# Routed experts: the first expert's weight remainders and token remainders placed anew on VectorE

## The chip, the cores and the metric

One core of a Trainium2 chip runs the whole program. The metric is the device time of one execution in microseconds (us); lower is better. The engines are TensorE (PE in the rows, with PEld for its weight loads), VectorE (DVE), ScalarE (ACT), GpSimd (POOL) and SyncE (SP), each with its own queue of instructions that runs in order.

## The reference

Sliding-window attention (8 batches, 8 heads, 576 positions, head size 64, window 64), and on its output a layer of 8 experts. Every expert takes exactly `cap` tokens, in the order of all token and expert scores:

```python
    logits = x @ w_gate
    order = np.argsort(-logits.flatten())
    for idx in order:
        tok, e = (int(idx) // E, int(idx) % E)
        if assigned[tok] >= 0 or counts[e] >= cap:
            continue
        assigned[tok] = e
        counts[e] += 1
...
    for e in range(E):
        mask = assigned == e
        h = np.maximum(x[mask] @ w1[e], 0.0)
        out[mask] = h @ w2[e]
```

There are N = 4608 tokens of D = 512, E = 8 experts with F = 1024 hidden values, and cap = 576.

## The kernel before

Attention runs first, to about 148 us. Then three streams of work share the engines. *Routing* finds, for one expert after another (position p = 0 to 7), which expert fills up next and the list of its 576 tokens: choice steps on VectorE (`choices`, L454 to L461), eight rounds of comparisons with thresholds (`compare`, L469) and counting matmuls (L538 for p = 0, L554 for later p), and then a list of token numbers, `idx` (L758). *Loading* brings the weights of expert p as eight tiles of 128 x 1024, four of w1 and four of w2 (`load`). *Products* are the matrix products.

Products are made to nearly float32 precision with numbers of a shorter kind (fp32r): each operand is a rounded part (`wh` for weights, `xh` for tokens, `hh` for hidden values) and a remainder (`wl`, `xl`, `hl`), and a product takes three matmuls, high by high, low by high and high by low. ScalarE makes the rounded parts (L899, L1002, L1156). The token and hidden remainders are subtractions on VectorE (L1006, L1161). A weight remainder is made in one of two ways: by a subtraction on VectorE (L903), or by ScalarE writing the negated rounded part (L908) and a DMA from GpSimd's queue that adds the weights to it in memory (L910). In expert 0 the first three tiles go the first way and the other five the second; experts 1 to 5 go the second way throughout.

The tokens of an expert are gathered from the attention's output by five indirect DMAs of GpSimd (L1012), four of 128 tokens and one of 64. TensorE transposes each gathered tile (L936), and ScalarE and VectorE make `xh` and `xl` of it. The first products are units: 128 hidden values by 256 or 320 tokens, twelve matmuls into one of three PSUM buffers (L1188), four of `wh` by `xh`, four of `wl` by `xh`, four of `wh` by `xl`. Expert 0 starts with six units on its first 256 tokens, which need token tiles 0 and 1; units 1 and 2 use weight tile 0, units 3 and 4 tile 1, units 5 and 6 tile 2. The second products (L1227, L1235) follow, and the results are scattered by GpSimd (L1217).

The order of all instructions is fixed while the kernel is built, by a planner with a clock of its own (`Streams`). Every stream is a generator; what it yields is a planned delay or a condition on which it is held, and it issues instructions when its time has come. `busy(dt, eng)` adds a planned duration to an engine's planned end and returns how far that end lies ahead. Routing paces itself on VectorE by

```python
    def dve(self, dt):
        return self.busy(0.4 * dt, "dve") + 0.6 * dt
```

so a routing step waits for all that is planned on VectorE, and each choice step is `yield self.dve(490)`. In the same clock (ns) a weight remainder on VectorE is 1130, a token remainder 600, a unit of 256 columns 1440, and a hidden remainder 335. The real engines follow the planned order, each at its own speed. With Z for the planner's time at which the first list is there, before the change: the gathers are issued at Z; the three weight tiles of expert 0 are converted at Z, Z+1.15 and Z+2.30 us and their remainders issued 1.05 after each; the transposes of token tile 0 are issued at Z+4.18 and of tile 1 at Z+5.46, `xh` 1 at Z+5.89 and `xl` 1 at Z+6.59.

The clock of TensorE has two levels here, and sparse work after attention leaves it on the lower one; `warm` issues matmuls whose results nobody uses (dummies): 28 behind the last step of the first list (L476, called at the end of `steps`), and 6 between the transposes of token tiles 0 and 1.

Of the kernel before, what the change touches and what calls it, by code (L numbers as in the profile page):

```python
# [9 lines left out]
FT = mybir.dt.float32  # L10
FR = mybir.dt.float32r
# [3 lines left out]
AF = mybir.ActivationFunctionType  # L15
OP = mybir.AluOpType
# [344 lines left out]
class Routing:  # L361
# [132 lines left out]
    def steps(self, p):  # L494

        nc, wk, V = self.nc, self.wk, self.V
# [6 lines left out]
        if p < E - 1:  # L503
# [19 lines left out]
            for r in range(NR):  # L523
# [18 lines left out]
                else:  # L542
# [22 lines left out]
                    st = self.st[0:M]  # L565
# [186 lines left out]
            for h in range(2):  # L752
                nc.tensor.matmul(ip[32 * g:32 * g + 32], ils[:, :, h], self.s5[:, h, g], start=(h == 0), stop=(h == 1))
        if p == 0:
            self.warm(28)
        yield self.busy(100) + 200 + slack
        idx = self.rt.tile([128, 5], U32, name=f"idx{p}")
        nc.vector.tensor_copy(idx, ip)  # L758
# [2 lines left out]
        if p < E - 1:  # L761
            if not p:
                nc.vector.scalar_tensor_tensor(self.eid, m, T[:, 0:1], best, op0=OP.is_gt, op1=OP.mult)
            eq = tile_([128, NJ], FT, name="eq", bufs=1)
            nc.vector.scalar_tensor_tensor(eq, Y[:, 1], CAP + 0.5, X[:, 1], op0=OP.is_lt, op1=OP.mult)  # L765
            nc.vector.scalar_tensor_tensor(self.eid, eq, code[:, 0:1], self.eid, op0=OP.mult, op1=OP.add)
            nc.vector.tensor_scalar(self.un, self.eid, 0.0, None, op0=OP.is_equal)
            yield self.dve(400)
            e1 = tile_([128, E], FT, name="e1")
            nc.vector.tensor_scalar(e1, self.cw, code, -FAR, op0=OP.is_equal, op1=OP.mult)  # L770
            nc.vector.tensor_tensor(V, V, e1[:, None, :].to_broadcast([128, NJ, E]), OP.add)
            yield self.dve(600)

            nc.vector.scalar_tensor_tensor(self.oh, m[:, :, None].to_broadcast([128, NJ, E]), T[:, 0:1], one,
                                           op0=OP.is_gt, op1=OP.mult)
            c2 = tile_([128, E], BF, name="c2")
            with nc.allow_low_precision(reason="whole numbers up to 36"):
                nc.vector.tensor_reduce(c2, self.oh.rearrange("p j e -> p e j"), axis=AX.X, op=OP.add)
            yield self.dve(900)

            def taken():
                cn = self.room(128, E)
                nc.tensor.matmul(cn, self.ones, c2, start=True, stop=True)
                yield self.busy(110) + 200 + slack
                nc.vector.tensor_tensor(self.left, self.left, cn, OP.add)
                e2 = tile_([128, E], FT, name="e2")
                nc.vector.tensor_scalar(e2, self.cw, code, -1.0e6, op0=OP.is_equal, op1=OP.mult)
                nc.vector.tensor_tensor(self.left, self.left, e2, OP.add)
                yield self.dve(500)

            self.taken = taken
            if not p or p == E - 2:
                yield slack if p < OWN else 1500
                yield from taken()

    def expert(self, p, code):
        ei = self.rt.tile([1, 1], I32, name=f"ei{p}")
# [19 lines left out]
class Experts:  # L817
# [30 lines left out]
    def load(self, p, ei):  # L848

        nc, fw = self.nc, self.fw  # L850
        yield lambda: self.taken == self.pairs[p]
        e = nc.sync.value_load(ei[0:1, 0:1], min_val=0, max_val=E - 1)
        eg = nc.gpsimd.value_load(ei[0:1, 0:1], min_val=0, max_val=E - 1) if p == 0 else None
        st, there = {}, {}

        def fetch(i):
            st[i] = fw.tile([128, 1024], FT, name="st", bufs=STAGE)

            q, r = (nc.gpsimd, eg) if p == 0 and i >= 4 else (nc.sync, e)
            q.dma_start(st[i], self.part(i, r))  # L860

            there[i] = max(self.clock(), there.get(i - 1, 0)) + \
                (LOAD if p else 1500) * (1 if i else 2)
            if q is nc.gpsimd:
                there[i] = max(there[i], self.clock() + self.busy(600, "pool") + 4700)

        ahead = 2 if p in SEVEN else 3 if p else 4
        for i in range(ahead):
            fetch(i)
        if p == 0:  # L870
            yield lambda: self.gathered

        def sums(x, y):
            w = x.rearrange("p (k c h f) -> p k c h f", k=2, c=2, h=2)
            s = y.rearrange("p (s c f) -> p s c f", s=4, c=2)
            tt = nc.vector.tensor_tensor
            for d, a, b, op in ((s[:, 0], w[:, 0, :, 1], w[:, 1, :, 1], OP.add),
                                (s[:, 2], w[:, 0, :, 0], w[:, 0, :, 1], OP.subtract),
                                (s[:, 1], s[:, 0], w[:, 0, :, 0], OP.subtract),
                                (s[:, 3], w[:, 1, :, 0], s[:, 1], OP.subtract)):  # L880
                tt(d, a, b, op)
                yield self.busy(350, "dve")

        seven = p in SEVEN
        jobs = [(i, k) for i in range(2 * NCH) for k in range(2 if seven and i < NCH else 1)]
        for i, k in jobs:
            if p == 0 and i == 3:
                yield lambda: self.tiles[0] > 1
            yield lambda: self.taken - self.ring < self.used
            if there[i] > self.clock():  # L890
                yield there[i] - self.clock()
            x = st[i]
            if k:
                x = fw.tile([128, 1024], FT, name="st", bufs=STAGE)
                yield from sums(st[i], x)
                yield 150
            hi = fw.tile([128, 1024], FR, name="wh", bufs=self.ring)
            lo = fw.tile([128, 1024], FR, name="wl", bufs=self.ring)
            nc.scalar.activation(hi, x, AF.Copy)  # L899
            yield self.busy(970, "act") + 80  # L900
            yield lambda: self.gathered > p
            if k and i < NCH - 1 or self.quick(p, i):
                nc.vector.tensor_tensor(lo, x, hi.bitcast(FT), OP.subtract)  # L903
                self.W[p, i, k] = (hi, lo)
                dt = self.busy(1130, "dve")
            else:

                nc.scalar.activation(lo, hi.bitcast(FT), AF.Copy, scale=-1.0)  # L908
                yield self.busy(970, "act") + 180
                nc.gpsimd.dma_start(lo.bitcast(FT), x, accum_op=OP.add)  # L910
                self.spawn(self.ready((p, i, k), hi, lo), self.busy(650, "pool") + ADDED - 1200)
                dt = 1300
            self.taken += 1
            if not k and i + ahead < 2 * NCH:
                fetch(i + ahead)
            yield max(100, dt - 1200) if p or i < 3 else 900
# [392 lines left out]
def body(tc, q, k, v, vt, wg, w1, w2, xs, out):  # L1309
    nc = tc.nc  # L1310
    with ExitStack() as ctx:
        cp = ctx.enter_context(tc.tile_pool(name="cp", bufs=1))
        ctx.enter_context(tc.manual_schedule())
        c = dict(identr=cp.tile([128, 128], FR, name="identr"))
        L = cp.tile([128, NJ, E], FT, name="L")
        rt = Routing(ctx, tc, c, L)
        with ExitStack() as actx:
            ap = actx.enter_context(tc.tile_pool(name="ap", bufs=1))
            c.update(consts(tc, ap))
            wgs = ap.tile([128, HP, 32], FT, name="wgs")  # L1320
            attention(actx, tc, c, q, k, v, vt, (wgs, wg), xs, L, lambda j0, j1: rt.choices(j0, j1, 0), rt.setup,
                      rt.counters)
        rt.start()
        ex = Experts(ctx, tc, c, xs, w1, w2, out)
        rt.spare = ex.room

        st = Streams()
        ex.spawn, ex.busy, rt.busy = st.add, st.busy, st.busy
        ex.clock = rt.clock = lambda: st.now
        ex.warm, ex.rows, rt.prime = rt.warm, rt.rows, ex.prime  # L1330

        def route():
            for p in range(E):
                for dt in rt.steps(p):
                    if p in rt.eint and p not in known:
                        known.add(p)
                        st.add(ex.load(p, rt.eint[p]))
                    if p in rt.idx and p not in listed:
                        listed.add(p)
                        st.add(ex.turn(p, rt.idx[p]))  # L1340
                    yield dt

        def products():
            for p in range(E):
                yield lambda: p in ex.XT
                yield from ex.steps(p, rt.idx[p])

        known, listed = set(), set()
        st.add(route())
        st.add(products())  # L1350
        st.run()
# [17 lines left out]
```

## Time and profile before

| what | us |
|---|---|
| median of 3 runs | 645.47 |
| lowest and highest run | 643.06, 645.69 |
| profiled execution, its time | 642.53 |
| profiled execution, its span | 640.8 |
| TensorE busy | 605.8 |
| VectorE busy | 460.5 |
| mean granted TensorE clock | 0.978 of full |

The span goes from the first to the last instruction of the profiled execution; its time also holds what lies around that. Busy time of TensorE is modelled, since matmuls overlap: a busy stretch is not a stretch at its peak. Idle time in brackets stands ahead of an instruction, with what ended it.

### The profile page before, as it was taken

The page shows a single profiled execution, that of the slowest core. Times are in us where ns is not written, and L with a number is a line of the kernel's source. Part 1 is how long each engine was busy: PE and PEld are TensorE (multiplying, and loading weights), DVE is VectorE, ACT ScalarE, POOL GpSimd, SP SyncE. Part 2 cuts the span into 40 slices and gives each one's busy share as a digit, 9 for nine tenths or more (in the row PEclk, how much of TensorE's full clock was granted, in tenths as well). Part 3 has the DMA queues.
Part 4 walks back from the last instruction along what each step waited for, and adds up shares of the span by engine and source line. Part 5 has one row for each costly group of instructions (what it writes and reads, how often), then busy time and mean ns, then how long its engine had stood idle before and what let it go on. Part 6 is the DMA issues. An engine that isn't in the chain of part 4 may idle for free. (4 is left out here: it accounts for less than half of the span.)

```text
span 640.8 us, 16975 instructions
## 1 busy us (share of the span) xinstructions
PE 605.8 (95%) x6423; PEld 523.7 (82%) x6423; DVE 460.5 (72%) x2036; ACT 340.7 (53%) x596; POOL 219.3 (34%) x231
## 2 busy tenths in 40 slices
PE   7899999995599999999999999999999999999995
PEld 6787887784489779978997898799789879889984
DVE  6887888877787768875877786778777954975610
ACT  2476677671255177255646448176437545666720
POOL 4454656450142062133306215132321515123211
PEclk9999999997599999999999999999999999999998
DMA  9997969991376098779669578868929828666711
GB/s 316 368 379 280 362 245 336 373 352 53 134 236 136 18 310 198 148 255 214 156 201 236 171 145 283 196 142 275 215 82 228 208 75 223 185 159 156 162 54 41
DMA packets 39761, 133.06 MB, mean 208 GB/s; under 512 B 5112, under 2 KB 5240, under 8 KB 39680
## 3 DMA queue, kind: packets, MB, share of 16 engines
q0 software_dynamic: 14992, 51.93, 35.0%
q1 hardware_dynamic: 24400, 79.52, 34.3%
q8 instruction: 51, 0.84, 0.5%
q10 hardware_dynamic: 288, 0.52, 0.3%
q14 instruction: 30, 0.25, 0.1%
HBM read 82.15 MB, written 18.87 MB: 158 GB/s over the span
## 5 line engine op out<-in xcount | busy, mean ns | idle before, releaser
L1217 POOL DMA_INDIRECT out<-ot,idx x40 | 41.3, 1033 | 197.0 <-ACT ot L1202 61.9
L1235 PE MATMUL o<-wh,hh 128*128 128x512 f32 x256 | 102.3, 400 | 0.4 <-ACT ot L1202 0.4
L1235 PE MATMUL o<-wl,hh 128*128 128x512 f32 x256 | 101.7, 397 | 0.0
L1235 PE MATMUL o<-wh,hl 128*128 128x512 f32 x256 | 101.2, 395 | 0.0
L144 POOL TENSOR_TENSOR st<-st,mx 128x512 f32<-128x512 f32 x72 | 73.4, 1040 | 67.1 <-DVE mx L137 60.5
L899 ACT ACTIVATE wh<-st 128x1024 fp32r<-128x1024 f32 x72 | 75.7, 1052 | 11.4 <-DMA st<-w 5.3
L910 POOL DMA_DIRECT2D wl<-st x59 | 54.4, 1091 | 70.9 <-ACT wl L908 47.7
L1156 ACT ACTIVATE hh<-h 128x256 fp32r<-128x256 f32 (+1 forms) x96 | 38.9, 407 | 65.7 <-PE h L1188 64.0
L1188 PE MATMUL h<-xh,wh 128*128 128x320 f32 (+1 forms) x384 | 69.9, 301 | 0.7 <-ACT xh L1002 0.7
L1188 PE MATMUL h<-xh,wl 128*128 128x320 f32 (+1 forms) x384 | 70.5, 299 | 0.0
L1188 PE MATMUL h<-xl,wh 128*128 128x320 f32 (+1 forms) x384 | 69.7, 299 | 0.4 <-DVE xl L1006 0.4
L137 DVE CUSTOM_DVE_ANT_0 st<-Sp,mask 128x128 f32<-128x128 f32 x288 | 67.1, 283 | 3.0 <-PE Sp L128 2.4
L1012 POOL DMA_INDIRECT xg<-xs,idx x40 | 44.0, 1100 | 72.0 <-DVE eq L765 62.0
L908 ACT ACTIVATE wl<-wh 128x1024 fp32r<-128x1024 f32 x59 | 62.3, 1056 | 0.8
L1202 ACT ACTIVATE ot<-o 128x512 f32<-128x512 f32 x34 | 20.3, 597 | 75.0 <-PE o L1235 63.5
L1188 PEld LDWEIGHTS h<-xh,wh 128*128 128x128 f32 x384 | 56.8, 189 | 1.4 <-ACT xh L1002 0.8
L1188 PEld LDWEIGHTS h<-xl,wh 128*128 128x128 f32 x384 | 56.9, 189 | 0.8 <-DVE xl L1006 0.6
L1188 PEld LDWEIGHTS h<-xh,wl 128*128 128x128 f32 x384 | 56.9, 189 | 0.2
L1235 PEld LDWEIGHTS o<-wh,hh 128*128 128x128 f32 x256 | 48.1, 188 | 10.5 <-ACT ot L1202 0.8
L1235 PEld LDWEIGHTS o<-wh,hl 128*128 128x128 f32 x256 | 48.1, 188 | 9.3
L1235 PEld LDWEIGHTS o<-wl,hh 128*128 128x128 f32 x256 | 48.2, 188 | 8.8
L152 ACT ACTIVATE pt<-Tp 128x512 f32<-128x512 f32 x72 | 39.7, 594 | 19.4 <-PE Tp L150 18.3
(237 smaller groups left out, 1255.0 us busy)
## 6 DMA issues: line engine op xcount, KB each, us to landing
st<-w SPq DMA_DIRECT2D x60, 512.0 KB, 6.4
wl<-st POOLq DMA_DIRECT2D x59, 512.0 KB, 6.1
V<-v SPq DMA_DIRECT2D x16, 584.0 KB, 9.3
xs<-x SPq DMA_DIRECT2D x36, 256.0 KB, 4.5
VT<-vt SPq DMA_DIRECT2D x8, 640.0 KB, 10.1
VT<-vt SPq DMA_DIRECT2D x8, 512.0 KB, 8.3
Q<-q SPq DMA_DIRECT2D x6, 640.0 KB, 6.8
K<-k SPq DMA_DIRECT2D x6, 640.0 KB, 7.8
```

The costliest lines, as they stand in the source:

```text
L137: nc.vector.tensor_tensor_reduce(st[:, h, :], Sp[h % 2][:, h // 2], mk, scale=-0.125, scalar=3.0e38, op0=OP.add, op1=OP.min, accum_out=mx[ ...
L144: nc.gpsimd.tensor_tensor(st, st, mx[:, :, None].to_broadcast([128, 4, 128]), OP.subtract)
L152: nc.scalar.activation(pt, Tp, AF.Exp, scale=-1.0)
L899: nc.scalar.activation(hi, x, AF.Copy)
L908: nc.scalar.activation(lo, hi.bitcast(FT), AF.Copy, scale=-1.0)
L910: nc.gpsimd.dma_start(lo.bitcast(FT), x, accum_op=OP.add)
L1012: nc.gpsimd.indirect_dma_start(out=g[0:n, a], out_offset=None, in_=self.xs, in_offset=IndirectOffsetOnAxis(ap=idx[0:n, a:a + 1], axis=0))
L1156: nc.scalar.activation(hh[:, f, c0:c1], h, AF.Relu)
L1188: nc.tensor.matmul(h, wv[:, cc, 128 * (f % 2):128 * (f % 2) + 128], xt[:, cc, c0:c1], start=(k == 0), stop=(k == 11))
L1202: nc.scalar.activation(ot, o, AF.Copy)
L1217: nc.gpsimd.indirect_dma_start(out=self.out, out_offset=IndirectOffsetOnAxis(ap=idx[0:m, a:a + 1], axis=0), in_=ot[0:m], in_offset=None)
L1235: nc.tensor.matmul(o, ht[:, f, 128 * a:128 * a + 128], wt[:, 512 * (f % 2):512 * (f % 2) + 512], start=(f == 0 and k == 0), stop=(f == NF ...
```

## The change

It touches only what happens around the start of expert 0. In `load`, weight tiles 0 and 1 of expert 0 get a piece of their own: both are converted on ScalarE, tile 1 first and then tile 0, without waiting between them; the remainder of tile 0 is issued on VectorE when the gathers have been issued, that of tile 1 a planned microsecond after the `xl` of the second token tile (`lows[0] > 1`). The loop then goes on with tile 2, so its conversion and its remainder come later too; tile 3 no longer waits for the second token tile. Routing is held, at the end of p = 0, on the condition `settled`, which is the same `lows[0] > 1`: the choice steps for expert 1 are issued behind the `xl` of the first two token tiles. And the dummies behind the first list go from 28 to 25.

```diff
--- before.py
+++ after.py
@@ -752,7 +752,7 @@
             for h in range(2):
                 nc.tensor.matmul(ip[32 * g:32 * g + 32], ils[:, :, h], self.s5[:, h, g], start=(h == 0), stop=(h == 1))
         if p == 0:
-            self.warm(28)
+            self.warm(25)
         yield self.busy(100) + 200 + slack
         idx = self.rt.tile([128, 5], U32, name=f"idx{p}")
         nc.vector.tensor_copy(idx, ip)
@@ -792,6 +792,8 @@
             if not p or p == E - 2:
                 yield slack if p < OWN else 1500
                 yield from taken()
+            if not p:
+                yield self.settled
 
     def expert(self, p, code):
         ei = self.rt.tile([1, 1], I32, name=f"ei{p}")
@@ -883,9 +885,27 @@
 
         seven = p in SEVEN
         jobs = [(i, k) for i in range(2 * NCH) for k in range(2 if seven and i < NCH else 1)]
+        if p == 0:
+            jobs = jobs[2:]
+            yield max(0, there[1] - self.clock())
+            hi, lo = ({}, {})
+            for i in (1, 0):
+                hi[i] = fw.tile([128, 1024], FR, name="wh", bufs=self.ring)
+                lo[i] = fw.tile([128, 1024], FR, name="wl", bufs=self.ring)
+                nc.scalar.activation(hi[i], st[i], AF.Copy)
+                yield self.busy(970, "act") + 80
+            yield lambda: self.gathered
+            for i in (0, 1):
+                if i:
+                    yield lambda: self.lows[0] > 1
+                    yield 1000
+                nc.vector.tensor_tensor(lo[i], st[i], hi[i].bitcast(FT), OP.subtract)
+                self.W[p, i, 0] = (hi[i], lo[i])
+                self.busy(1130, "dve")
+                self.taken += 1
+                fetch(i + ahead)
+                yield 100
         for i, k in jobs:
-            if p == 0 and i == 3:
-                yield lambda: self.tiles[0] > 1
             yield lambda: self.taken - self.ring < self.used
             if there[i] > self.clock():
                 yield there[i] - self.clock()
@@ -1322,7 +1342,7 @@
                       rt.counters)
         rt.start()
         ex = Experts(ctx, tc, c, xs, w1, w2, out)
-        rt.spare = ex.room
+        rt.spare, rt.settled = ex.room, lambda: ex.lows[0] > 1
 
         st = Streams()
         ex.spawn, ex.busy, rt.busy = st.add, st.busy, st.busy
```

## Rows read from the trace of the kernel before

**Rows 1.** The page, busy time of TensorE: us, share, instructions
```profile
PE 605.8 (95%) x6423; PEld 523.7 (82%) x6423; DVE 460.5 (72%) x2036; ACT 340.7 (53%) x596; POOL 219.3 (34%) x231
```

**Rows 2.** Timeline of TensorE, 172 to 187: start, us, line, operation, count, idle before
```profile
172.80 4.84 PE L476 MATMUL rps<-r,ones 128*128 128x288 bf16 x28
177.70 0.17 PE L783 MATMUL rps<-c,ones 128*128 128x8 bf16 x1
178.12 0.52 PE L936 MATMUL tp<-identr,xg 128*128 128x128 f32 x4 [0.26 <-DMA xg<-xs,idx]
...
180.36 0.74 PE L1188 MATMUL h<-xh,wh 128*128 128x256 f32 x4 [0.69 <-ACT xh L1002]
180.94 0.64 PE L1188 MATMUL h<-xh,wl 128*128 128x256 f32 x4
182.01 0.39 PE L1188 MATMUL h<-xl,wh 128*128 128x256 f32 x1 [0.44 <-DVE xl L1006]
...
186.54 0.43 PE L554 MATMUL rps<-G,one 128*32 128x60 bf16 x9
```

**Rows 3.** Timeline of VectorE over the same stretch
```profile
174.48 1.22 DVE L903 TENSOR_TENSOR wl<-st,wh 128x1024 fp32r<-128x1024 f32 x1
...
178.32 1.22 DVE L903 TENSOR_TENSOR wl<-st,wh 128x1024 fp32r<-128x1024 f32 x1
179.46 0.44 DVE L454 TENSOR_REDUCE m<-L 128x36 f32<-128x288 f32 x1
...
181.28 0.68 DVE L1006 TENSOR_TENSOR xl<-tp,xh 128x512 fp32r<-128x512 f32 x1
...
184.33 0.47 DVE L469 TENSOR_TENSOR G<-m,tab 128x300 bf16<-128x300 f32 x1
```

**Rows 4.** Timeline of ScalarE, the second first-expert weight tile
```profile
174.69 1.06 ACT L899 ACTIVATE wh<-st 128x1024 fp32r<-128x1024 f32 x1 [0.24 <-DMA st<-w]
```

**Rows 5.** Timeline of GpSimd: gathers of expert 0, then of expert 1
```profile
174.70 1.83 POOL L1012 DMA_INDIRECT xg<-xs,idx  x1 [0.30 <-issue]
...
229.88 1.01 POOL L1012 DMA_INDIRECT xg<-xs,idx  x1 [3.45 <-DVE eq L765]
...
236.26 1.02 POOL L910 DMA_DIRECT2D wl<-st  x1
```

**Rows 6.** Timeline of TensorE where expert 0 ends and expert 1 begins
```profile
242.05 0.79 PE L936 MATMUL tp<-identr,xg 128*128 128x128 f32 x8
242.67 0.47 PE L1235 MATMUL o<-wh,hl 128*128 128x512 f32 x1
...
243.44 0.43 PE L554 MATMUL rps<-G,one 128*128 128x60 bf16 x9
...
244.03 0.63 PE L1188 MATMUL h<-xh,wh 128*128 128x256 f32 x4
244.50 0.64 PE L1188 MATMUL h<-xh,wl 128*128 128x256 f32 x4
```

**Rows 7.** DMA issues from 236.0 to 236.9: engine, count, size, us to landing
```profile
wl<-st POOLq DMA_DIRECT2D x1, 512.0 KB, 4.8
```

**Rows 8.** Windows of 1 us: busy PE, PEld, DVE, ACT, POOL, clock, DMA
```profile
148.00:149.00 1.00, 0.00 (x0) 0.09 (x1) 0.86 (x7) 0.05 (x1) 0.00 (x0) 1.00 0.06 23
...
150.00:151.00 1.00, 0.00 (x0) 0.00 (x0) 0.90 (x6) 0.00 (x0) 0.00 (x0) 1.00 0.47 184
...
152.00:153.00 1.00, 0.25 (x5) 0.10 (x1) 0.56 (x3) 0.00 (x0) 0.00 (x0) 0.50 0.00 0
...
174.00:175.00 1.00, 1.00 (x6) 0.64 (x5) 0.96 (x3) 0.76 (x2) 0.69 (x2) 0.50 0.95 365
175.00:176.00 1.00, 1.00 (x8) 0.73 (x7) 1.00 (x2) 0.78 (x2) 1.00 (x1) 0.82 1.02 418
```

**Rows 9.** Timeline, GpSimd and TensorE, where expert 2 begins
```profile
290.26 3.75 POOL L910 DMA_DIRECT2D wl<-st  x4
...
302.30 0.64 PE L1188 MATMUL h<-xh,wh 128*128 128x256 f32 x4
```

## Prediction, made before the changed kernel ran

> **What bounds the kernel.** I read the page first, then the timeline of each engine from the first expert's token list to the end of its products, then the joints between experts. TensorE is busy 605.8 of 640.8 us [rows 1], and behind the wait before 182.01 its timeline marks none up to 245, through the joint of experts 0 and 1 [rows 2, 6]. So a microsecond that TensorE loses or wins between 172 and 245 reaches the end of the kernel nearly whole, and one that another engine wins is worth nothing unless TensorE was waiting for it.
>
> The reader should see three things. First, the start: 28 dummies run to about 177.64, the matmul of L783 follows, and the transposes of the first token tile wait for the gather to land at 178.12, with 0.26 us idle; then TensorE waits 0.69 us for `xh` and later for `xl` [rows 2]. Second, what makes `xl` late: VectorE does the third weight remainder at 178.32 and the first choice step of expert 1 at 179.46, and comes to the second `xl` only at 181.28 [rows 3]. Third, the joint: expert 1's first unit starts at 244.03, and its weight remainder, needed at 244.50, was sent off by GpSimd at 236.26, right behind the five gathers that began at 229.88 [rows 5, 6]. It took 4.8 us [rows 7], so it lay there at 241.1, with 3.4 us to spare.
>
> **The change, part by part.**
>
> *Fewer dummies.* 28 dummies take 4.84 us, 0.173 each; three fewer end 0.52 us sooner. Behind them stand L783 and the first transposes, which wait for the gather anyway [rows 2]. The 0.26 us of idle time becomes some 0.8. Cost and gain 0, if the clock stays up. The clock is at half speed at 174, and 0.82 in the mean from 175 to 176, behind the 28 dummies and what ran before them [rows 8]; three dummies from the end still leave more than a microsecond of work after it rose. I take 0. The other bound: if the clock fell, a stretch at half speed like that of the dummies (172.80 until within 175 to 176) would cost half its length, 1.1 to 1.6 us.
> The Trainium skill, "TensorE: Matmul & The Clock Gate", section "Why this matters for your kernels", says that gaps of idle time between matmul bursts put TensorE back to the half clock, which speaks against fewer dummies. The trace agrees in kind: TensorE did nothing in two of the three microseconds from 148 to 151 at clock 1.00, and was at 0.50 from 152 to 153 [rows 8]. By the rule the sum would be up to 1.6 us worse; by the rows on the dummies, 0.
>
> *First weight tiles.* ScalarE now converts tile 1 first (it starts at 174.69, when the tile is there [rows 4]) and tile 0 after it, 1.06 us each, so `wh` 0 is ready at 176.8 instead of 174.5 and its remainder runs from about 176.9 to 178.1. The first use of `wl` is 180.94 [rows 2]: hidden, with 2.8 us to spare. In VectorE's queue only the counting of L785 to L788 stands behind it, which nobody near waits for.
> The second gather took 1.83 us beside a weight remainder at 174.48; the first gather of expert 1 took 1.01 without one [rows 3, 5]. At 0.8 us for each, and with one remainder beside the gathers where three were, the last gather ends about 1.6 us sooner, an estimate. The transposes of tile 0 hang on the first gather, which was over before the first remainder began, and those of tile 1 followed the six dummies without a wait. Gain 0; upper bound 0.65 us, the six dummies' length, if tile 1 was in fact on the edge.
>
> *`xl` first.* Remainder 2 and the choices go behind the second `xl`. It can then start when `xh` 1 is done, just before the first unit's 180.36, and end at 181.04 (0.68). The eight matmuls before it are issued by 181.42 (0.58 for the first four, 0.48 for the next), so the wait up to 182.01 goes: gain 0.59, the marked idle part being 0.44 [rows 2]. I take 0.55. Remainder 1 then runs at 181.5 to 182.7, for a use at about 185; remainder 2 (ScalarE after `xh` 2, VectorE to 185.0) is used at about 188. Both hidden.
>
> *What is late next.* VectorE now idles from 178.6 to 179.3 and takes up two remainders, 2.4 us, and all choice steps in its fullest stretch. Expert 1's routing is what slips, and the order of the instructions is fixed by the planner, so I work its clock by hand, from Z, when the token list is there.
> Before: choices begin at Z+5.30; the six steps (each waits for VectorE's planned backlog) end at Z+9.17, two comparisons and a pause later the first counting matmul of L554 is put at Z+10.68. The third unit has then given nine of its twelve matmuls, and there L554 stands in the trace, at 186.54 [rows 2].
> After: the steps are put at Z+6.59, 7.68, 9.21, 11.47, 13.20 and 14.07, since remainder 1 (7.59), remainder 2 (8.74), four `xl` and four `hl` are queued with them, 1.13, 1.13, 0.60 each and 0.34 each in the planner's prices. The counting matmul comes at Z+15.90, six matmuls into the seventh unit (it starts at Z+15.37). That is 5.2 us later by the planner; in matmuls it is 3 + 36 of 0.12 and 6 of about 0.15 (320 columns for 256), 5.6 us. Less the 0.55 gained, expert 1's routing is 5.0 us later on the chip. The eight rounds are paced by the same steps in both kernels, so I carry 5.0 to the token list, bounds 3.5 and 6.
>
> *The joint.* Expert 1's gathers begin at 229.88 + 5.0, its first weight remainder lands at 241.1 + 5.0 = 246.1, and TensorE needs it at 244.50. That is 1.6 us late. Besides, work that stood before 244.50 is still to do: the transposes of tiles 2 and 3 (0.62, from 242.05 to 242.67) and one counting matmul (0.43) [rows 6]. Loss 1.6 + 1.0 = 2.6 us net of the early gain; with the bounds of the delay, 1.1 to 3.6.
> At expert 2 it does not come again: the remainders are sent at 290.26 and its first unit starts at 302.30, 12 us later, against 8 us at expert 1 [rows 5, 6, 9]. A routing that is about 2.4 us later against the products still fits.
>
> **Sum.** Dummies 0, first weights 0, `xl` and the joint +2.6. The profiled execution took 642.53 us (span 640.8 and 1.7 around it), 2.9 below the median of the three runs, which themselves lie 643.06 to 645.69. I put the sum on the mean of the four executions, 644.2: 646.8 us. On the profiled one alone it would be 645.1.
>
> **The rivals.**
>
> *The delay is taken up.* The rounds catch up by 2 us or the remainder lands sooner (at expert 1 it had 3.4 us to spare), and the early gain alone is left: 644.2 - 0.6 = 643.6. For it: a later round runs beside the longer units, and the planner's delay is only as good as its constants. Against it: in the trace L554 stands where the plan puts it.
>
> *The clock falls at the joint (the other side: slower).* Expert 0's products would end at about 241.3 and the remainder lands at 246.1; between them TensorE has only two tiles' transposes (0.62), a counting matmul (0.43) and four matmuls (0.47), 1.5 us in 4.8 [rows 6]. That is like the stretch from 148 to 151, after which it was at 0.50 [rows 8]. A stretch at half speed as behind 172.80 then costs 1.1 to 1.6 us more: 2.6 + 1.5 = 4.1, 648.3. It decides from a delay of about 5 us on, where the gap is as empty as that stretch was.
> The skill's rule on gaps, cited above, speaks for this one; no stretch here shows such a gap from full clock with matmuls on either side.
>
> *A real gain.* Tile 1 was on the edge (0.65), the `xl` wait goes (0.55), and the order of the later experts, which is planned anew, loses some of its waits, 2 of the 35 us in which TensorE is not busy [rows 1]. All together 3.2, 641.0. Nothing in the profile ties the last part to this change.
>
> **How the numbers follow.** About 0.5%, 3.2 us, is what a measurement of this kernel can tell from no change. Late joint without the clock, 0.38 (0.04 of it over 3.2); joint with the clock, 0.20; a clock that falls behind the fewer dummies besides, 0.02; taken up, 0.32; real gain, 0.08. Slower by over 0.5%: 0.04 + 0.20 + 0.02 = 0.26. Faster: 0.08. Within: 0.34 + 0.32 = 0.66. The likeliest case's own range is 645.3 to 647.8; the range over the cases, with the two microseconds by which executions of one kernel differ here, is 642.2 to 650.0.
>
> **What would show it.** In the changed kernel: 25 dummies, then some 0.8 us idle before the transposes; no wait for `xl` near 181.5; two weight remainders on VectorE after 181; the first L554 near 191.4 inside the seventh unit; the token list of expert 1 near 234.4; and a gap of TensorE before expert 1's first `wl` matmul. I am wrong if the list comes before 232.5, if TensorE has no gap at the joint, or if its clock there or at 180 is 0.50 without my having given it the most weight.

## The result, and the profile after

The changed kernel takes 651.53 us in the median of 6 runs (650.2 to 652.16), against 644.43 for the kernel before (6 runs, 643.06 to 645.69): a ratio of 1.0104, 95% interval 1.0088 to 1.012. It is slower by 7.1 us. 646.8 had been forecast, with a range that ended at 650.0.

The profiled execution has a span of 649.8 us, 9.0 more than that of before. The loss has two places. The list of expert 0 comes at 175.72 in place of 172.93, so 2.8 us were gone before any changed instruction ran; that part is told in the last section. In the twelve profiles that this document draws on, that list comes between 172.17 and 175.72, so the start of one execution says little about the medians; of the 7.1 us between them, what lies behind the list is what can be placed. From there on the kernel loses another 6.1 us. The table gives the time between the first matmuls of each stretch, read from the timeline of TensorE, in us:

| stretch | before | after | difference |
|---|---|---|---|
| list of expert 0 to its first unit | 7.43 | 7.78 | +0.35 |
| expert 0, first products | 32.82 | 31.43 | -1.39 |
| expert 0, second products | 30.85 | 31.66 | +0.81 |
| expert 1, first products | 28.56 | 34.62 | +6.06 |
| expert 1, second products | 29.71 | 30.06 | +0.35 |
| from expert 2 to TensorE's last instruction | 331.47 | 331.43 | -0.04 |

So, on balance, all of it arises while expert 1's first products run.

The start first. Timeline of TensorE in the changed kernel (start, us, line, operation, count, idle before), to be held against [rows 2]:

```profile
175.59 5.19 PE L476 MATMUL rps<-r,ones 128*128 128x288 bf16 x25
180.83 0.17 PE L783 MATMUL rps<-c,ones 128*128 128x8 bf16 x1
181.25 0.52 PE L956 MATMUL tp<-identr,xg 128*128 128x128 f32 x4 [0.26 <-issue]
...
184.07 0.64 PE L1208 MATMUL h<-xh,wl 128*128 128x256 f32 x4
184.55 0.29 PE L1208 MATMUL h<-xl,wh 128*128 128x256 f32 x1
...
194.25 0.43 PE L554 MATMUL rps<-G,one 128*32 128x60 bf16 x9
```

The wait for `xl` is gone: the first `xl` matmul at 184.55 directly follows the `wl` ones. L554 stands at 194.25, inside the seventh unit. Less the 2.79 us by which this execution came later to the list, that is 191.46, where 191.4 had been worked out. But 25 dummies took 5.19 us here, more than 28 did before, because the clock rose later against them, and the transposes follow the dummies and not the gather. In windows of 1 us (busy PE, PEld, DVE, ACT, POOL, then the granted clock, DMA share, GB/s) the clock is still 0.50 from 178 to 179, with dummies since 175.59, and rises only in the next window:

```profile
178.00:179.00 1.00, 1.00 (x6) 0.64 (x5) 0.43 (x1) 1.00 (x2) 0.69 (x2) 0.50 1.01 414
179.00:180.00 1.00, 1.00 (x8) 0.67 (x6) 0.69 (x1) 0.22 (x1) 0.81 (x1) 0.70 1.00 283
```

Timeline of VectorE over the same stretch, against [rows 3]:

```profile
179.31 1.23 DVE L902 TENSOR_TENSOR wl<-st,wh 128x1024 fp32r<-128x1024 f32 x1 [0.88 <-DMA st<-w]
...
183.48 0.69 DVE L1026 TENSOR_TENSOR xl<-tp,xh 128x512 fp32r<-128x512 f32 x1 [0.35 <-ACT xh L1022]
184.08 0.44 DVE L454 TENSOR_REDUCE m<-L 128x36 f32<-128x288 f32 x1
184.44 1.22 DVE L902 TENSOR_TENSOR wl<-st,wh 128x1024 fp32r<-128x1024 f32 x1
...
186.75 1.23 DVE L923 TENSOR_TENSOR wl<-st,wh 128x1024 fp32r<-128x1024 f32 x1
```

The order is as planned: one remainder ahead of the `xl`, two behind them, and the choice steps (L454) behind the second `xl`.

The joint, TensorE in the changed kernel, against [rows 6]:

```profile
244.81 0.86 PE L956 MATMUL tp<-identr,xg 128*128 128x128 f32 x8
246.59 0.74 PE L1208 MATMUL h<-xh,wh 128*128 128x256 f32 x4 [0.91 <-ACT xh L1022]
247.55 0.75 PE L1208 MATMUL h<-xh,wl 128*128 128x256 f32 x4 [0.23 <-DMA wl<-st]
...
248.97 0.81 PE L956 MATMUL tp<-identr,xg 128*128 128x128 f32 x8
...
250.41 0.43 PE L554 MATMUL rps<-G,one 128*128 128x60 bf16 x9
```

The late remainder is there, but costs 0.23, and 0.91 goes to waiting for `xh`, which comes late because the transposes now stand right in front of the first unit. The transposes of tiles 2 and 3 and one counting matmul come behind the first unit, as worked out.

What had not been foreseen comes some ten microseconds later. ScalarE, first the kernel before and then the changed one:

```profile
251.25 0.44 ACT L1156 ACTIVATE hh<-h 128x320 fp32r<-128x320 f32 x1 [0.43 <-PE h L1188]
252.33 1.06 ACT L899 ACTIVATE wh<-st 128x1024 fp32r<-128x1024 f32 x1 [0.64 <-DMA st<-w]
```

```profile
253.36 0.39 ACT L1176 ACTIVATE hh<-h 128x256 fp32r<-128x256 f32 x1 [0.16 <-PE h L1208]
257.77 1.06 ACT L919 ACTIVATE wh<-st 128x1024 fp32r<-128x1024 f32 x1 [4.02 <-DMA st<-w]
258.74 0.42 ACT L1176 ACTIVATE hh<-h 128x320 fp32r<-128x320 f32 x1
...
260.82 1.06 ACT L919 ACTIVATE wh<-st 128x1024 fp32r<-128x1024 f32 x1 [0.72 <-DMA st<-w]
```

The conversion of expert 1's seventh weight tile stands in ScalarE's queue and waits 4.02 us for the tile to land. Before, the same instruction waited 0.64. Behind it in the queue are the `hh` evacuations, which take TensorE's results out of PSUM, and VectorE waits 4.15 us for them. TensorE of the changed kernel goes on until it needs what they give (timelines of VectorE, then of TensorE):

```profile
259.19 0.42 DVE L1181 SCALAR_TENSOR_TENSOR hl<-h,hh 128x256 fp32r<-128x256 f32 x1 [4.15 <-ACT hh L1176]
```

```profile
258.40 0.75 PE L1208 MATMUL h<-xl,wh 128*128 128x320 f32 x4
259.89 0.71 PE L1208 MATMUL h<-xh,wh 128*128 128x256 f32 x4 [0.74 <-DVE dg L560]
...
263.23 0.58 PE L554 MATMUL rps<-G,one 128*128 128x60 bf16 x9 [2.04 <-DVE G L469]
```

It loses 0.74 and 2.04 us, the second in front of a counting matmul of the routing, whose mask stands behind the late `hl` in VectorE's queue. Then its clock falls. Windows of 1 us, with the columns as above:

```profile
262.00:263.00 1.00, 0.00 (x0) 0.00 (x0) 0.76 (x3) 1.00 (x2) 0.00 (x0) 1.00 1.03 205
...
265.00:266.00 1.00, 1.00 (x5) 1.00 (x5) 0.90 (x6) 0.00 (x0) 0.00 (x0) 0.50 1.11 221
...
267.00:268.00 1.00, 1.00 (x6) 1.00 (x6) 0.71 (x3) 0.25 (x1) 0.00 (x0) 0.50 1.01 201
268.00:269.00 1.00, 1.00 (x9) 1.00 (x8) 0.16 (x1) 0.00 (x0) 0.00 (x0) 0.82 1.05 209
```

What the clock falls short of 1.00, summed over the windows from 264 to 269, is 1.71 us. Stalls 2.78, clock 1.71, the wait of 0.23 for the late remainder and the deferred transposes 0.65 make 5.4 of the 6.06; the rest lies among the product matmuls. The deferred counting matmul is no part of it: six groups of L554 stand in this stretch in both kernels, and the one more is found in expert 1's second products.

Why the tile is late is told by the DMA queue of SyncE, which waits for `wl` transfers. The two answers are the waits of SP from 225 to 262 in the kernel before and from 231 to 252 in the changed one (total us, times, longest):

```profile
SPq L860 <- DMA wl<-st: 17.2, 2, 14.5
```

```profile
SPq L862 <- DMA wl<-st: 16.1, 2, 14.0
```

A weight tile may be fetched into one of six buffers. The seventh takes that of the first, which is free when the first tile's remainder (a transfer by GpSimd that reads `st`) has landed, and this one is queued behind the gathers, which wait for the token list. In the kernel before that remainder landed at 241.1 [rows 5, 7], and the fetch was issued at 241.15. The chain, step by step:

| | before | after |
|---|---|---|
| list of expert 1 | 229.44 | 236.00 |
| first remainder sent | 236.26 | 242.83 |
| seventh tile's fetch issued | 241.15 | 247.63 |
| ScalarE takes the tile | 252.33 | 257.77 |
| expert 1's first unit | 244.03 | 246.59 |
| ScalarE comes to the conversion | 251.69 | 253.75 |

From the list to the tile it is 22.9 us before and 21.8 after. From the first unit to the point where ScalarE asks for it, 7.66 and 7.16. But from the list to the first unit it is 14.6 before and 10.6 after: the list has come 4.0 us nearer to the products. 0.64 that it waited before, and 4.0, and 0.5 earlier asked, less 1.1 faster arrival, is 4.0.

### The profile page after: what moved, and what is told of

Same layout as the page of the kernel before. It is cut to its first block, busy times and chain, and to the rows that moved or that the text cites. A ratio compares the mean times of both kernels' runs of the same rounds, so it can differ in the third digit from the quotient of the medians.

```text
span 649.8 us, 16974 instructions
## 1 busy us (share of the span) xinstructions
PE 609.8 (94%) x6420; PEld 527.8 (81%) x6420; DVE 460.5 (71%) x2036; ACT 340.9 (52%) x596; POOL 214.7 (33%) x231
## 5 line engine op out<-in xcount | busy, mean ns | idle before, releaser
L919 ACT ACTIVATE wh<-st 128x1024 fp32r<-128x1024 f32 x70 | 73.5, 1052 | 10.1 <-DMA st<-w 7.3
L1032 POOL DMA_INDIRECT xg<-xs,idx x40 | 39.9, 997 | 76.5 <-DVE eq L765 52.3
L1181 DVE SCALAR_TENSOR_TENSOR hl<-h,hh 128x256 fp32r<-128x256 f32 x96 | 40.2, 419 | 15.4 <-ACT hh L1176 15.1
```

The lines of the kernel that those rows point to most:

```text
L1032: nc.gpsimd.indirect_dma_start(out=g[0:n, a], out_offset=None, in_=self.xs, in_offset=IndirectOffsetOnAxis(ap=idx[0:n, a:a + 1], axis=0))
L1181: nc.vector.scalar_tensor_tensor(t, h[:, a - c0:b - c0], 0.0, hh[:, f, a:b].bitcast(FT), op0=OP.max, op1=OP.subtract)
```

## The experiments

All ratios are against runs of the kernel before on the same chip. The question was at first which part of the change carries the loss, then by which chain.

**The change without the hold.** Weight part and 25 dummies stay:

```diff
-            if not p:
-                yield self.settled
```

> The change without the hold on routing (the choices for expert 1 are issued as soon as the counting of expert 0 is done). Theory A (the hold and the full stretch of VectorE make expert 1's routing late, and its gathers, its weight remainders and the weight tiles behind them): the list of expert 1 comes 56 to 57 us after the list of expert 0 as before, instead of 60.3, no stall at 259 to 263, and the time is that of the kernel before, 643 to 645 us. Theory B (the new place of the weight remainders costs the time): it stays near 651.

650.06 us (10 runs), ratio 1.0068, 1.0042 to 1.0093. Some of the loss goes, most does not.

**The hold alone** in the kernel before:

```diff
+            if not p:
+                yield self.settled
...
-        rt.spare = ex.room
+        rt.spare, rt.settled = ex.room, lambda: ex.lows[0] > 1
```

> The kernel before with the hold on routing alone; weight tiles and 28 dummies as before. Theory A: part of the loss, since the choices begin 1.3 us later but one weight remainder only stands behind the second token remainder: list of expert 1 some 58 us after the first, 645 to 648. Theory B: no loss, 644, less up to 0.6 for the earlier token remainder.

648.61 us (10 runs), ratio 1.0052, 1.003 to 1.0073. So neither part is innocent, and putting the loss on one of them, as both theories did, was wrong. In the profile of the hold alone the list of expert 1 comes 49.09 us behind expert 0's first unit, as before (49.08); in the one without the hold 50.59, of which 1.7 is a half-clock stretch at 182 to 186. Only both together make the list later against that unit (52.5). But against expert 1's first unit it comes nearer with either part alone, 13.5 us ahead of it in both profiles in place of 14.6 (with the hold alone because expert 0's products got shorter by as much), and ScalarE comes to the seventh tile too early. ScalarE in the kernel with the hold alone:

```profile
249.75 0.38 ACT L1158 ACTIVATE hh<-h 128x256 fp32r<-128x256 f32 x1
250.03 1.05 ACT L910 ACTIVATE wl<-wh 128x1024 fp32r<-128x1024 f32 x1
253.65 1.06 ACT L901 ACTIVATE wh<-st 128x1024 fp32r<-128x1024 f32 x1 [2.57 <-DMA st<-w]
```

The tile comes 22.9 us behind the list, as in the kernel before; the conversion now stands behind three `hh` of the 256-column units, where before a 320-column one came in between. The order is planned anew when any instruction moves, and this conversion had no slack for it: 0.64 that it waited before, 1.06 by which the list came nearer and 0.87 earlier asked are the 2.57. The wait was 2.49 us without the hold. TensorE lost 1.15 us (hold alone) and 1.07 us (without the hold) behind it, in front of L554.

That is not all that the two kernels lose. Expert 1's first products took 30.34 and 30.27 us against 28.56, and expert 6's took 24.58 and 24.46 against 22.38, which is more; expert 6 comes back below. Without the hold TensorE also waited 2.06 us for `xh` before expert 0's first unit (0.69 before), ahead of the half-clock stretch at 182.

**28 dummies in the changed kernel.**

```diff
-            self.warm(25)
+            self.warm(28)
```

> The change with 28 dummies instead of 25. Theory C (fewer dummies cost, by the clock at the start): it gains against the change, 649 or less. Theories A and B: same as the change, 651 to 652.5, up to 0.7 us more where the dummies run at half clock and hold the first transposes back.

654.54 us (4 runs), ratio 1.0153, 1.0102 to 1.0205. Giving the dummies back gains nothing. The wait for the seventh tile is there (4.80 us), as is the half-clock stretch behind it. The time is at or above the upper end of what was expected, 651 to 653.2, on a chip on which the kernel before took 645.73; in the profile expert 6's first products took 26.84 us, with a second half-clock stretch in them at 557.

**25 dummies in the kernel before**, the other side of that question:

```diff
-            self.warm(28)
+            self.warm(25)
```

> The kernel before with 25 dummies in place of 28, and nothing else. As predicted (the dummies are hidden): the first transposes still wait for the gather, the first unit starts about 7.4 us after the list as in before, up to 8.6 where the clock rises late whatever the number of dummies, and the time is that of before within 0.5 us (645.7 on the chip of the first runs). Rival, the emptier stretch lets the clock fall: a stretch at 0.50 within 10 us after the list, the first unit some 1.7 us later, 647.4.

644.25 us (10 runs), ratio 0.999, 0.997 to 1.001. The dummies are worth nothing either way here. The first unit came 7.93 us behind the list; with 28 dummies it came 7.43 to 8.60 behind it, in five profiles of the kernel before and of its variants.

**The seventh tile's conversion planned 6 us later**, in the changed kernel, all else as it is:

```diff
         for i, k in jobs:
             yield lambda: self.taken - self.ring < self.used
+            if p == 1 and i == 6 and not k:
+                yield 6000
```

> The change with one edit more: the conversion of the seventh weight tile of expert 1 (and so the eighth behind it) is planned 6 us later, so that ScalarE does not stand at the head of its queue waiting for the tile. Theory A1 (the 2.8 us of stall at 259 to 263 and the half clock after it come from that wait on ScalarE): the stall and the half clock go, 4 to 5 us less than the change, 646 to 648. Theory A2 (the products themselves lack the weights): the time stays near 651, the wait only moves.

ScalarE, where it took the seventh tile:

```profile
258.44 0.44 ACT L1178 ACTIVATE hh<-h 128x320 fp32r<-128x320 f32 x1 [1.32 <-PE h L1210]
258.78 1.05 ACT L921 ACTIVATE wh<-st 128x1024 fp32r<-128x1024 f32 x1
```

Three evacuations went ahead of it, the conversion found its tile there and waited for nothing, TensorE's two stalls are gone and the clock stays up there. Expert 1's first products took 29.82 us in place of 34.62. So the wait of ScalarE is shown to be the cause of the loss in that stretch. The time was 649.66 us (10 runs), ratio 1.0058, 1.0029 to 1.0087, where 646 to 648 was expected: by the ratios some 3 us were won, less than the 4.8 that this stretch gave back. In the profile expert 6's first products took 28.05 us, with two half-clock stretches from 550 to 558 that cost 3.42.

**The first remainder ahead of the gathers**, to test the chain and not only its end. For expert 1 the remainders need not wait until the gathers are issued; one remainder then goes in front of them, and the rest of GpSimd's order is otherwise the same:

```diff
-            yield lambda: self.gathered > p
+            yield lambda: self.gathered > (0 if p == 1 else p)
```

> The changed kernel with one remainder of expert 1 (that of weight tile 0) sent off by GpSimd ahead of expert 1's gathers in place of behind them, which the condition on the gathers before the remainders does. The order is otherwise the same. A, the seventh weight tile is late because its buffer is that of tile 0, which comes free only when this remainder is done: ScalarE's wait of 4.02 us for the seventh tile goes to under 1, the waits of TensorE of 0.74 and 2.04 us and the stretch at half clock behind them go, and so does the wait of 0.23 for the remainder at the joint; expert 1's first products take 30 us in place of 34.6, and the time is 4 to 5 us below that of the changed kernel, 646.5 to 647.5. B, the tile is late because its own transfer is slow beside the gathers: the wait stays at 3 to 4 us, the first products at 34 to 35, 651.

647.46 us (10 runs), ratio 1.0042, 1.002 to 1.0064. GpSimd, and then ScalarE, in that kernel:

```profile
232.15 0.96 POOL L930 DMA_DIRECT2D wl<-st  x1 [1.08 <-ACT wl L928]
233.42 1.25 POOL L1032 DMA_INDIRECT xg<-xs,idx  x1 [0.30 <-DVE e L770]
...
239.69 1.03 POOL L930 DMA_DIRECT2D wl<-st  x1
```

```profile
249.78 1.05 ACT L919 ACTIVATE wh<-st 128x1024 fp32r<-128x1024 f32 x1
...
255.36 1.06 ACT L919 ACTIVATE wh<-st 128x1024 fp32r<-128x1024 f32 x1 [2.76 <-DMA st<-w]
```

The seventh tile was fetched at 241.46 and taken at 249.78 without a wait, so its buffer did hang on that remainder. But now the eighth waits 2.76 us: its buffer is that of the second tile, whose remainder still goes behind the gathers (239.69), and its fetch was issued at 247.85. I had expected the waits to go; the chain has a second link of the same kind. The remainder gained less than its place says: it was sent 7.0 us sooner against the list, but took 9.2 us to land in place of 4.8, so the fetch came 2.5 us sooner. TensorE lost one stall of 1.79 in place of two and kept its clock, and expert 1's first products took 31.20 us. Ahead of them 1.2 us went back: the gathers now come behind the remainder, the transposes waited 1.06 us for them, and expert 0's second products took 32.87 us in place of 31.66.

**The same, and the last expert's gathers earlier.** In all the changed kernels so far, expert 6's first products took longer (23.9 to 28 us against 22.4; in the changed kernel itself the stretch before them was 1.4 us shorter, so little of it is left there in sum). The order on GpSimd had changed there as well: the fifth write of expert 5's rows came ahead of expert 7's gathers, where before the gathers had been first.

```diff
-            yield 10000
+            yield 4000
```

> The run before (the remainder of tile 0 ahead of the gathers) with the last expert's gathers also put ahead of the last-but-one write of an expert's rows, as in the kernel before, by a pause of 4000 in place of 10000. C, the longer first products of expert 6 (23.9 to 28 us after the changes against 22.4) come from that order on GpSimd: they go to 22.4 to 23, and the time is 1 to 2 us below the run before, 645.5. D, they come from VectorE being late with the sums of expert 5 for another reason, or from the clock: they stay at 24 or more, and the time is that of the run before.

GpSimd and TensorE in the kernel without this edit:

```profile
540.53 1.01 POOL L1237 DMA_INDIRECT out<-ot,idx  x1 [2.14 <-DMA out<-ot,idx]
541.85 1.03 POOL L1032 DMA_INDIRECT xg<-xs,idx  x1 [0.30 <-issue]
...
548.62 1.03 POOL L930 DMA_DIRECT2D wl<-st  x1
```

```profile
554.73 0.53 PE L1074 MATMUL h<-xh,wl 128*128 128x288 f32 x2 [1.37 <-DMA wl<-st]
```

and GpSimd with it:

```profile
536.33 1.03 POOL L1032 DMA_INDIRECT xg<-xs,idx  x1 [0.30 <-issue]
...
542.58 1.03 POOL L930 DMA_DIRECT2D wl<-st  x1
543.90 1.03 POOL L1237 DMA_INDIRECT out<-ot,idx  x1 [0.30 <-issue]
```

The write waits 2.14 us for an earlier write, with five gathers and a remainder queued behind it, and the remainder is what TensorE waits for. With the gathers first, the remainder goes 6 us sooner, the wait is gone, and expert 6's first products took 22.41 us. 645.66 us (10 runs), ratio 1.0022, 0.9999 to 1.0045. In this kernel the whole change is still in place, and with two orders on GpSimd altered it is 1.2 us above the kernel before in place of 7.1. The last step is 1.8 us between two medians whose intervals overlap, and its cause rests on one profile of each kernel.

**The hold with both orders**, on the kernel before (pause 8000):

```diff
+            if not p:
+                yield self.settled
...
-            yield lambda: self.gathered > p
+            yield lambda: self.gathered > (0 if p == 1 else p)
...
-            yield 10000
+            yield 8000
```

> The kernel before with the hold of the choices alone (the second remainder of expert 0's tokens ahead of them), the remainder of expert 1's tile 0 ahead of its gathers, and the last expert's gathers in the order of the kernel before. If the two losses found (the late seventh tile, the last gathers) were all that the hold cost, the time is that of before less the wait for the second remainder (0.59) and the deferred work: 645 to 645.7, no slower than before, at best 0.6 faster. If the hold costs anything else, 647 to 648.6 as with the hold alone.

643.22 us (10 runs), ratio 0.9982, 0.9955 to 1.001.

**The two orders without the hold**, and **the kernel above once more**:

```diff
-            yield lambda: self.gathered > p
+            yield lambda: self.gathered > (0 if p == 1 else p)
...
-            yield 10000
+            yield 8000
```

> The kernel before with only the two orders on GpSimd that the runs found: the remainder of expert 1's tile 0 ahead of its gathers, and a pause of 8000 that leaves the last expert's gathers where they were. No part of the change is in it. If the hold of the choices has a gain of its own (the wait for the second remainder, 0.59 us, and a counting matmul deferred), this kernel takes the time of before, 644.5 less at most 0.3, and the run with the hold is 0.6 to 1.3 below it. If the gain of the run with the hold came from the new order on GpSimd, the two take the same time.

> The same kernel as the one with the hold and the two orders on GpSimd, in more runs. 0.998 of before was measured with an interval that reaches 1.001. If the hold's gain is real the ratio stays at 0.997 to 0.999 and the interval ends below 1; if not, it is 1.000.

Without the hold 645.34 us (12 runs), ratio 1.0001, 0.9978 to 1.0023. With it, in 12 more runs, 645.27 us, ratio 1.0014, 0.9988 to 1.0039. So the 0.998 is no gain that was shown. Expert 0's first products were shorter with the hold (32.22 and 32.12 us, against 32.82 before and 33.06 without it), by the 0.6 to 0.9 that the wait for `xl` had cost, and the end of the kernel shows nothing of it: in the second profile expert 6's first products took 23.72 us, against 22.57 in the first. That is one kernel with the gathers first, and in the second profile TensorE waits 0.67 us for the remainder all the same; so of the 1.6 us by which the earlier gathers shortened that stretch, a part may be what executions differ by. No version was measurably faster than the kernel before.

## Why the prediction was wrong, point by point

- **Dummies, 0.** Right: 0.999 by themselves. One reason was not: that the first transposes "wait for the gather anyway" held for the one execution read. Where the clock rises later the dummies end later and hold the transposes (181.25 behind 180.83), so their end is hidden only in some executions. In the three of the twelve profiles in which the half clock behind the attention lasted 23.9 us the first transposes waited for the gather; in the nine in which it lasted 27.3 they followed the dummies, with 25 and with 28 of them. The 0.8 us of idle time foreseen ahead of them was 0.26.
- **First weight tiles, 0.** Right as a price on TensorE at the start: neither the first `wl` nor the transposes made it wait. The gathers took 1.01, 1.06, 0.95, 1.24 and 0.93 us, and the last ended 1.85 us sooner behind the list, where 1.6 was estimated. The slowest lies beside the weight remainder at 179.31, but 0.95 does in part too, and one of expert 1's took 1.19 before with no remainder beside it; so the price of 0.8 for each is not shown.
- **`xl` first, -0.55.** Right: the wait is gone, and the hold without the weight part shortens expert 0's first products by 0.6 to 0.9.
- **The delay of the routing, 5.0, bounds 3.5 to 6.** The start of it was right to 0.1 us (L554), in part by luck: L554 stands three matmuls into the seventh unit and not six, which is some 0.45 us sooner, and the first unit came 0.35 later behind the list than before, which was not foreseen. Carrying it unchanged through eight rounds was too much: from list to list it came to 3.8, and 3.4 against the first unit. So the rival "The delay is taken up" came in part, and with it the remainder at the joint was hardly late; the time went the other way.
- **The joint, 1.6 late and 1.0 deferred.** Right in kind, less in size: the remainder cost 0.23, and 0.91 went to a wait for `xh` that was not foreseen; of the deferred work the transposes cost 0.65 in expert 1's first products, and the counting matmul moved on to the second ones.
- **The step that failed** is in "What is late next" and "The joint": the late list was priced at one reader. They followed the list to the first remainder and to the joint's `wl`, which had 3.4 us to spare, and stopped there. The same remainder also frees the buffer of the seventh weight tile, SyncE fetches the tile behind it, and ScalarE, whose queue is in order, stands for it with the evacuations behind. That reader had nothing to spare: the kernel before already showed 0.64 us of waiting at 252.33, a row that the prediction left out, because TensorE marked no idle time there. So each microsecond by which the list came nearer to the products was added to that wait, and 2.78 us of 4.02 reached TensorE, with a half-clock stretch of 1.71 behind them. These 4.5 us stood at nothing in the sum of +2.6; behind the list 6.1 was measured. The conversion later in the plan took the stalls away (34.62 to 29.82); the remainder earlier moved the wait from the seventh tile to the eighth.
- **"At expert 2 it does not come again."** Right: from expert 2 to the end the two profiles differ by 0.04 us in sum, though inside it expert 6's first products lose 1.5 and the stretch before them gains 1.4.
- **The rival of the clock.** The clock fell, but behind the stalls at 259.89 and 263.23 and not in the gap of the joint; it cost 1.71 where 1.1 to 1.6 was estimated. By the row: TensorE did nothing from 262 to 263 and was at 0.50 from 265. The Trainium skill, "TensorE: Matmul & The Clock Gate", section "Why this matters for your kernels", says that idle gaps between bursts of matmuls bring the half clock back; the trace agrees in kind. The rival was given 0.20, at the joint, and there the changed kernel kept its clock. In the kernel with both orders it did fall there: 0.50 for 3.41 us from 244.72, behind waits of TensorE of 0.29 and 0.91 at 241.81 and 243.92.
- **The basis, 644.2.** Right: 644.43 in six runs.
- **The range, 642.2 to 650.0.** Its lower end lies above the 641.0 of the rival "a real gain", though that had a chance; the time missed the other end, by 1.5.

## What to carry to other kernels

When something becomes later, list every reader of it, and every reader of the buffers that those free: here the late list reached a remainder, its staging buffer, a fetch, and through a conversion in an in-order queue the evacuations of TensorE's results. Look for waits that exist already on engines that are off the path; a wait of 0.64 us that costs nothing is a chain without slack, and a delay is added to it in full. In a kernel whose order is planned from prices, moving a few instructions in one stage reorders the queues of later stages too (here at expert 1 and expert 6), so compare each queue's order, and not only the edited place.

## What the runs showed of the hardware

Each single fall of the clock among the products and in the attention cost the same 1.71 us by the granted clock, 0.50 for 3.41 us: in the changed kernel from 19 to 23, 118 to 122 and 264 to 269, in the kernel with the earlier gathers from 244 to 249, without the hold from 182 to 186. Each came behind a gap of TensorE. TensorE of the changed kernel, at the first two:

```profile
17.74 0.87 PE L128 MATMUL Sp<-K,Q 64*64 64x128 f32 x19 [2.10 <-issue]
```

```profile
116.56 0.45 PE L128 MATMUL Sp<-K,Q 64*64 64x128 f32 x8 [2.22 <-issue]
```

Those at 19 and 118 lie in the attention part, which no edit touches: TensorE was idle for 2.10 us before 17.74 and for 2.22 us before 116.56, put down to "issue", where the kernel before was idle for 1.15 and 0.25 at the same instructions and kept its clock. What makes these gaps longer in one execution than in another is open. VectorE's rows (`r<-r`) show what they came to. The changed kernel's execution lags by 2.19 us behind the first (39.42 for 37.23), by 0.39 at 57, so that most of it was made up within the attention, by 0.75 ahead of the second (112.57 for 111.82) and by 2.79 behind it (132.18 for 129.39). So about 2 of the 2.8 us that were lost before the list come with the second gap and its half clock. How much of what runs of one kernel differ by comes from such falls is open: in the six runs of the changed kernel the mean granted clock goes from 0.969 to 0.977, and the time does not follow it: 651.46 and 652.16 at 0.969, 651.60 at 0.977.

Also open is what made expert 6's first products slower in the changed kernel itself: there TensorE waited 2.05 us for `hh` from VectorE at 555.43, and not for the remainder. With the first remainder ahead of the gathers and the order at expert 6 still as in the changed kernel, that wait was 0.57, so this order alone does not make it.
